# A new order table for a gated-linear-attention and spatial-gating kernel on one core

## Chip, core and metric

One core of a Trainium2 chip runs the kernel. The metric is the device time of one execution in microseconds (us). The kernel before took 139.16 us, the median of 3 runs (138.14 to 139.8). The profile is one execution of it, with a span of 137.9 us from the first to the last instruction, at a granted TensorE clock of 1.000.

Engines are named as the profile names them: PE is TensorE (matmuls), PEld its weight loads, DVE VectorE, ACT ScalarE, POOL GpSimd, and SP the engine that issues nearly all DMAs.

## What is computed

A recurrent attention is followed by a gated layer with a projection in, a spatial mix over the sequence and a projection out. Batch 4, 8 heads, sequence 768, head dimension 48, so the model dimension is 384; the hidden dimension is 1024, half of it gate.

```python
for t in range(S):                                   # _attn_ref
    state = alpha[:, :, t, :, None] * state + np.einsum('bhd,bhe->bhde', k[:, :, t], v[:, :, t])
    y[:, :, t] = np.einsum('bhd,bhde->bhe', q[:, :, t], state)
...
h = np.maximum(x @ w_in, 0.0)                        # _moe_ref, x = y with the heads side by side
u, v = (h[..., :d_ff // 2].copy(), h[..., d_ff // 2:].copy())
v_n = (v - mu) / np.sqrt(var + 1e-06)
v_s = np.einsum('ts,bsd->btd', w_spatial, v_n) + b_spatial[None, :, None]
gated = u * v_s
return (gated @ w_out).astype(np.float32)
```

## The kernel before

The sequence is cut into chunks of 128 positions, 6 to a batch and 24 in all. Inside a chunk the recurrence is written as matmuls. ACT takes the logarithm of alpha (`ln`, `lns`), PE sums it along the chunk with triangular matrices (`half`, `cum`, `cums`), ACT takes the exponential of both signs (`einv`, `eexp`), and k and q are multiplied by these (`kt` on POOL or DVE, `qt` on DVE). PE turns k and q round (`tr`, `trk`), ACT or DVE copies them out of PSUM (`ev`, `evs`), PE makes the scores (`sc`), DVE masks them (`ms`, two a chunk), and PE makes the chunk's output (`y`), adding the old state's share. The state goes from chunk to chunk by `upd` (PE), `z` (DVE), `S` (POOL or DVE) and `sb` (its bf16 copy). Chunks come in three shapes: fours (`four_chunks`, chunks 0 to 3 and 6 to 9), a pair (`pair`, chunks 4 and 5) and singles (`single`, the rest).

Each chunk's output is copied out of PSUM (`xe`). After it come, batch by batch, the projections `v` and `u` on PE with `ve` and `ue` behind them (the copies with relu), the layer norm (`bn` and `nm` on DVE, `rs` on ACT, `vn` on DVE or ACT), the spatial mix `s` (PE, in two parts of 4 and 2 matmuls, since the last two of its six row blocks come late), `se` (DVE, adds the bias), `g` (times u), the projection out `o` (PE, 4 matmuls of 384 columns), `oe` (out of PSUM) and `st` (the store). A `u`, `v`, `s` or `o` takes one PSUM bank until its reader is done with it; there are 8 banks.

The order of all this is written by hand. Every function above makes no instructions when it is called; it records operations with `op(key, engines, emit, deps, take, use)`. There are 944 of them, numbered in the order of recording. The table `PLAN` (lines 42 to 88) then says in which order and on which engine they are emitted, and `replay` (line 109) walks it. A word like `P62@0:512#0:512#0` means: operation 62 on PE, with bank 0 for the slot that it takes, and ahead of it two fillers (`warm`, line 239), matmuls of constants (`junk`) of 512 columns into bank 0, whose results nobody reads. The letters P, D, A, G and S stand for PE, DVE, ACT, POOL and SP. Each engine's words, read in the order of the table, are its program; it runs them strictly in that order, and an instruction whose inputs aren't there holds up all behind it on that engine. DMAs are issued in the order of SP's words. An operation's choice among engines is a letter of the table too.

```python
for x in junk:
    cols, kind, n = re.fullmatch("([0-9]+)([#~=])([0-9]+)", x).groups()
    ...
    warm(int(cols), int(n), kind)
...
op.emit(eng)
```

The lines that the prediction's steps touch: 242 (the fillers), 682 (`ln` of the first four chunks), 717 and 700 (`half`, `cum` and the chunk totals there), 740 and 743 (`einv`, `eexp` there), 725 (`ebc`, the exponentials of the totals), 189 (the products `kt`, `qt`, `S`, `g`), 393 (`z`), 843 and 949 (`ms`), 1067 and 1068 (`bn`), 1096 (`vn` on DVE), 178 and 180 (copies on ACT and on DVE or POOL), 184 and 186 (copies with relu on ACT and on DVE), and 1005 (all matmuls of `v`, `u`, `s` and `o`).

Of the kernel before, what the change touches and what calls it, by code (L numbers as in the profile page):

```python
# [42 lines left out]
D2 D0 D4 D1 G9 G11 G5 G6 D3 S56 S57 S59 S58 A60 S12 S169 S170 A61 S275 S171 D8 P62@0:512#0:512#0:512#0 P66@1 P67 P63  # L43
P70@2 P71 P74@3 P75 A68 A64 D79 G82 P91@4,5 P52@6 A69 A72 A76 G7 A78 A92 A84 A65 G88 G87 A73 A77 D85 D90 D81 D93 D53
D83 D80 P103@6,4,5,7:512#7:424#7 P94@0,1 D86 D104 D89 D106 G13 P97@6,2:192#2 D98 A95 P100@3,0 D101 A96 P117@3,6:376#1
P115@4,1 A99 G107 G14 A15 A173 D102 D109 P128@0,2 D119 D118 P174@5 A116 A122 A176 P130@6,4 S16 D132 D131 S172 A135
P175@1 A129 P120@3 P54@2 G110 G105 P136@0,4 A121 A178 A55 G111 G108 P133@6 G181 A180 A134 G184 A179 D112 A177 D138
P123@7,3 P141@2 S20 G279 G280 G281 G17 G19 G18 D124 D125 P151@6 P187@7,4 P126@3 S23 S277 S276 D185 A152 A127 G186 G183
G113 G114 D182 P190@5,6 A189 A192 A142 P144@3 D137 P139@4 D188 D191 A140 G22 G21 D153 D143 P199@6,5 P196@2,7 P162@4
A283 A145 P290@0 A163 P154@1 P160@3 A282 A291 A155 D200 D201 D198 D197 D164 P193@4 A161 P156@7 A157 A165 D194 D146  # L50
P158@5 A159 G195 P202@1,2 P203 S26 A204 A147 D166 P293@4 P37@5,7 D38 P34@3,6 G24 S278 S387 S399 G25 S506 S29 D35
P207@1 D148 D208 D36 A39 A292 P205 P284@7 P40@3,5 A206 A285 A167 G10 D42 P210@2 D149 D150 D41 S388 S389 D168 D209 S401
S400 P287@5 P223@6 P219@3 P221@1 A211 A294 A224 A288 D212 A286 A220 A213 D298 D304 A289 A295 D214 D222 D215 A216
P225@6 P233@2 P217@3 P229@7 P237@0 A218 A28 D301 G300 G27 D307 G297 P226 D227 G303 G306 P43@3,5 D45 P230 P234 D231
D235 A296 A44 P46@4,6 P309@5,1 D311 P238 P49@7,3 D50 D51 A48 A47 A310 P312@2,6 P318@1,4 P315@5,7 P249@3 P250 A313 A319
# [1209 lines left out]
```

## Time and profile before

| what | value |
|---|---|
| median of 3 runs | 139.16 us (138.14 to 139.8) |
| span of the profiled execution | 137.9 us |
| median less span | 1.26 us |
| PE busy | 130.1 us (94%) |
| DVE busy | 120.2 us (87%) |
| ACT busy | 107.7 us (78%) |
| POOL busy | 86.6 us (63%) |
| last instruction on PE ends | about 134.3 us |

The profile gives the span of the execution that it took and no device time of its own; the difference of 1.26 us to the median is used as what lies around the span. "Busy" counts a matmul up to its modelled end, so PE can be counted busy through short waits. A row of the timeline gives the start in us from the span's start, the time that the merged instructions cover, the engine and line, the operation, and what it writes and reads; in brackets stands the engine's idle time just before and what ended it. A row of a table by stage gives the stage, its length, and for each engine its busy time and number of instructions.

### The profile page before, as it was taken

To read this page: it belongs to the slowest core of one execution; us is meant where nothing else is said; L and a number is where in the kernel's file an instruction comes from. 1 tells how busy PE (TensorE), PEld (TensorE's weight loads), DVE (VectorE), ACT (ScalarE), POOL (GpSimd) and SP (SyncE) were. 2 spreads that over 40 slices of the span, in tenths; PEclk is the share of its full clock that TensorE was granted. 3 is DMA by queue.
4 is the path that set the end of the run, shared out by engine and by line. 5 is a ranking of instruction groups with operands and counts; after the bars stand their busy time and mean duration, and the time that the engine had idled before them with its cause. 6 is when DMAs were issued, how large, how long until landed. Compare 5 with 4: busy or idle time off the path is not lost.

```text
span 137.9 us, 5298 instructions
## 1 busy us (share of the span) xinstructions
PE 130.1 (94%) x2108; PEld 79.4 (58%) x2122; DVE 120.2 (87%) x300; ACT 107.7 (78%) x261; POOL 86.6 (63%) x146
## 2 busy tenths in 40 slices
PE   6999998999999999799999999999999999999990
PEld 3365555565566556466657676656576765566560
DVE  6259999989989999899899999997999999974960
ACT  3476998999999799699997989999865796953040
POOL 7355899993499799761079989520799841004550
PEclk9999999999999999999999999999999999999999
DMA  3999999499989788699999898999960597101064
GB/s 88 370 372 381 344 349 361 106 373 382 355 162 281 159 168 165 124 186 188 193 204 201 164 209 156 189 186 216 213 134 5 187 349 270 63 0 57 0 233 172
DMA packets 76521, 28.66 MB, mean 208 GB/s; under 512 B 63056, under 2 KB 74960, under 8 KB 76496
## 3 DMA queue, kind: packets, MB, share of 16 engines
q1 hardware_dynamic: 76464, 28.32, 77.8%
q8 instruction: 16, 0.26, 0.8%
q14 instruction: 9, 0.07, 0.2%
q0 software_dynamic: 32, 0.00, 0.0%
HBM read 23.60 MB, written 4.72 MB: 205 GB/s over the span
## 4 chain that ended last, share of the span: by engine, by line
PE 60%; DMA 19%; POOL 8%; issue 3%; SPq 3%; ACT 3%; DVE 0%; POOLq 0%; ACTq 0%
PE bank L1005 43%; DMA raw_w<-in_moe_w_spatial_dram 6%; DMA kc<-in_k_dram 5%; DMA raw_w<-in_moe_w_out_dram 4%; DMA ac<-in_alpha_dram 4%; PE bank L960 3%; SPq L883 3%; PE bank L944 2%; PE bank L988 2%; PE bank L416 2%; POOL w_row L180 2%; POOL kt L189 2%; PE bank L932 1%; PE bank L898 1%; POOL state L189 1%
## 5 line engine op out<-in xcount | busy, mean ns | idle before, releaser
L1005 PE MATMUL bank<-w_spT,vn 128*128 128x384 bf16 x192 | 35.6, 327 | 0.0
L189 POOL TENSOR_TENSOR gT<-vs,uT 128x384 bf16<-128x384 f32 x28 | 25.7, 933 | 14.1 <-DVE vs L1152 14.1
L189 POOL TENSOR_TENSOR kt<-kc,binv 128x384 bf16<-128x384 f32 x22 | 20.2, 928 | 22.3 <-ACT binv L908 15.2
L1005 PEld LDWEIGHTS <-vn 128*128 128x128 bf16 x192 | 17.5, 98 | 11.2 <-issue 0.3
L1005 PE MATMUL bank<-w_in,xT 128*128 128x512 bf16 x58 | 17.4, 380 | 1.6 <-ACT xT L178 0.7
L1005 PE MATMUL bank<-xT,w_in 128*128 128x384 bf16 x96 | 18.7, 326 | 0.0
L1005 PE MATMUL bank<-w_out_sb,gT 128*128 128x384 bf16 (+1 forms) x100 | 18.4, 320 | 0.0
L1152 DVE TENSOR_TENSOR vs<-bank,bsp_bc 128x384 f32<-128x384 f32 x31 | 16.3, 549 | 2.4 <-PE bank L1005 2.3
L949 DVE TENSOR_TENSOR ptm<-bank,mask 128x512 bf16<-128x512 f32 x28 | 17.9, 682 | 0.5 <-PE bank L944 0.3
L178 ACT COPY kqT<-bank 128x512 bf16<-128x512 bf16 (+1 forms) x20 | 15.0, 793 | 3.1 <-PE bank L988 1.9
L1067 DVE BATCH_NORM_STATS2 stats<-v_sb 128x6 f32<-128x512 bf16 x24 | 16.4, 683 | 0.6 <-ACT v_sb L184 0.5
L184 ACT ACTIVATE v_sb<-bank 128x512 bf16<-128x512 f32 x20 | 11.7, 597 | 2.0 <-PE bank L1005 1.7
L184 ACT ACTIVATE uT<-bank 128x384 bf16<-128x384 f32 x27 | 12.4, 494 | 0.7 <-PE bank L1005 0.6
L1005 PEld LDWEIGHTS <-w_in 128*128 128x128 bf16 x96 | 9.0, 97 | 6.7 <-DVE ptm L949 0.3
L189 DVE TENSOR_TENSOR qt<-qc,bank 128x384 bf16<-128x384 f32 x24 | 12.6, 545 | 0.2 <-DMA qc<-in_q_dram 0.2
L1005 PEld LDWEIGHTS <-gT 128*128 128x128 bf16 x100 | 9.2, 98 | 5.8
L178 ACT CAST xT<-bank 128x384 bf16<-128x384 f32 x23 | 10.4, 482 | 1.1 <-PE bank L416 0.8
L843 DVE TENSOR_TENSOR ptm<-bank,mask 128x512 bf16<-128x512 f32 x16 | 10.3, 683 | 0.2 <-PE bank L836 0.2
L242 PE MATMUL bank<-junk 128*128 128x512 f32 (+3 forms) x14 | 8.8, 763 | 1.0 <-DVE junk L1231 1.0
L1005 PEld LDWEIGHTS <-xT 128*128 128x128 bf16 x72 | 6.2, 97 | 6.2 <-ACT xT L178 1.2
L178 ACT COPY raw_w<-bank 128x384 f32<-128x384 f32 x8 | 3.8, 479 | 7.3 <-PE bank L1005 7.2
L393 DVE TENSOR_TENSOR zs<-bank,state 128x384 f32<-128x384 f32 x16 | 8.8, 548 | 0.5 <-PE bank L932 0.4
(162 smaller groups left out, 264.3 us busy)
## 6 DMA issues: line engine op xcount, KB each, us to landing
ac<-in_alpha_dram SPq DMA_DIRECT2D x14, 192.0 KB, 4.4
kc<-in_k_dram SPq DMA_DIRECT2D x14, 192.0 KB, 4.4
qc<-in_q_dram SPq DMA_DIRECT2D x14, 192.0 KB, 4.4
vc<-in_v_dram SPq DMA_DIRECT2D x14, 192.0 KB, 4.2
raw_w<-in_moe_w_spatial_dram SPq DMA_DIRECT2D x3, 768.0 KB, 7.8
out_dram<-raw_w SPq DMA_DIRECT2D x11, 192.0 KB, 2.1
out_dram<-o_sb SPq DMA_DIRECT2D x9, 192.0 KB, 2.0
ac<-in_alpha_dram SPq DMA_DIRECT2D x2, 768.0 KB, 6.7
```

What stands on the lines that cost most here:

```text
L178: nc.scalar.copy(out=out, in_=in_)
L184: nc.scalar.activation(out=out, in_=in_, func=AF.Relu)
L189: ENG[eng].tensor_tensor(out=out, in0=in0, in1=in1, op=ALU.mult)
L242: nc.tensor.matmul(out=banks[n][:, 0:cols].rearrange("p (a b) -> p a b", a=4), lhsT=junk, rhs=junk[:, None, 0:cols // 4].to_broadcast([128 ...
L393: lambda _: nc.vector.tensor_tensor(out=zs[i % 3], in0=tp(), in1=state[(i - 1) % 3], op=ALU.add),
L843: nc.vector.tensor_tensor(out=ptm[n2][:, ci, s], in0=banks[sl.bank].rearrange("p (hp t) -> p hp t", hp=HP), in1=mask[:, 3][:, None, :].to_ ...
L883: nc.sync.dma_start(out=t[x].rearrange("p hp s d -> p (hp s) d"), in_=src[b, :, c * C:c * C + C, :].rearrange("h s d -> s h d"))
L949: nc.vector.tensor_tensor(out=ptm[n2][:, ci, s], in0=banks[sl_p[s].bank].rearrange("p (hp t) -> p hp t", hp=HP), in1=mask[:, 2][:, None, : ...
L960: nc.tensor.matmul(out=place(to, 3 * hp + (0, 1, 1, 2)[x]), lhsT=heads(vb, hp, x), rhs=ptm[n2][:, ci, x // 2, hp, :], start=(turn == 0), s ...
L1005: nc.tensor.matmul(out=ps, lhsT=lhsT, rhs=rhs, start=first and n == 0, stop=last and n == len(pairs) - 1)
L1067: nc.vector.bn_stats(out=stats[tt % 2], in_=v_sb[n2][:, tt, :])
L1152: nc.vector.tensor_tensor(out=vs[d], in0=banks[sl.bank][:, 0:TH], in1=bsp_bc[:, th, :], op=ALU.add)
```

## The change

`PLAN` is replaced as a whole. No operation is added or removed and none is computed differently: the same 944 operations, 265 words on PE and 99 on SP in both. What differs is the order on each engine, the banks, the fillers, and the engine of some operations. In the new table DVE has 232 operations in place of 235, ACT 240 in place of 234, POOL 108 in place of 111. Of these, `ve` (v's copy with relu) is on ACT 23 times in place of 20, `sb` 6 times in place of 2, `oe` 20 times in place of 18; DVE gets two more `vn` (20 for 18), two more `ue` (7 for 5), one `xe` and one weight cast more, and gives up two `oe`, two `we`, one `ev` and one `evs`; the copies of the triangle matrices (`triq`) go from DVE to POOL.

The core of the diff, its first lines and the fillers:

```diff
 PLAN = """
-D2 D0 D4 D1 G9 G11 G5 G6 D3 S56 S57 S59 S58 A60 S12 S169 S170 A61 S275 S171 D8 P62@0:512#0:512#0:512#0 P66@1 P67 P63
...
-D83 D80 P103@6,4,5,7:512#7:424#7 P94@0,1 D86 D104 D89 D106 G13 P97@6,2:192#2 D98 A95 P100@3,0 D101 A96 P117@3,6:376#1
...
+D3 S56 S57 G11 G9 D4 D1 D0 A60 G5 G8 P62@0:512#0:512#0:512#0:512#0:512#0:264#0 P70@1 P66@2 D2 A61 P67 A68 P63 A64 P71
...
+P103@4,6,7,5:512#7:512#7:208#7 A78 D104 D80 G7 D106 P97@1,2 D98 P100@3,4:232#3 S169 A173 A99 G107 A102 P94@0,2 A96 D95
```

Three places show what the change moves. A row names the line, the operation, what it writes and reads, and the columns; numbers behind names tell tiles of one kind apart (`bank_64` to `bank_71` are the 8 PSUM banks, `binv_106` to `binv_109` the exponentials for `kt` of the first four chunks' four row groups).

The first is PE at the very start. Before, three fillers stand ahead of the first sums of the logarithms:

```order
L242 MATMUL bank_64<-junk 128x512 x3
L717 LDWEIGHTS le_quad
L717 MATMUL bank_64<-la_100,le_quad 128x384
L717 LDWEIGHTS lt_quad
L717 MATMUL bank_64<-la_100,lt_quad 128x384
L717 LDWEIGHTS le_quad
L717 MATMUL bank_65<-la_100,le_quad 128x384
```

Now there are five and a half of them, and what goes second into a bank of its own (65) is row group 2's sum in place of row group 1's:

```order
L242 MATMUL bank_64<-junk 128x512 x5
L242 MATMUL bank_64<-junk 128x264
L717 LDWEIGHTS le_quad
L717 MATMUL bank_64<-la_100,le_quad 128x384
L717 LDWEIGHTS lt_quad
L717 MATMUL bank_64<-la_100,lt_quad 128x384
L717 LDWEIGHTS le_quad
L717 MATMUL bank_65<-la_100,le_quad 128x384
```

The second place is ACT just behind these sums: `einv` (L740), `eexp` (L743), `ebc` (L725) and the copies of k (`kqT`). Before:

```order
L740 ACTIVATE binv_107<-bank_65 128x384
L740 ACTIVATE binv_106<-bank_64 128x384
L743 ACTIVATE bank_65<-bank_65 128x384
L740 ACTIVATE binv_108<-bank_66 128x384
L740 ACTIVATE binv_109<-bank_67 128x384
L725 ACTIVATE bcq_121<-bank_67 64x16 x2
L178 COPY kqT_110<-bank_68 128x4x2x64
L178 CAST o_sb_156<-vc 128x384
L743 ACTIVATE bank_64<-bank_64 128x384
L743 ACTIVATE bank_66<-bank_66 128x384
L743 ACTIVATE bank_67<-bank_67 128x384
```

Now one more exponential stands ahead of the last `einv`, and `ebc`, which stood right behind it, stands sixth behind it:

```order
L740 ACTIVATE binv_107<-bank_66 128x384
L740 ACTIVATE binv_106<-bank_64 128x384
L740 ACTIVATE binv_108<-bank_65 128x384
L743 ACTIVATE bank_65<-bank_65 128x384
L743 ACTIVATE bank_66<-bank_66 128x384
L740 ACTIVATE binv_109<-bank_67 128x384
L178 CAST o_sb_156<-vc 128x384
L178 COPY kqT_111<-bank_70 128x4x2x64
L743 ACTIVATE bank_67<-bank_67 128x384
L178 COPY kqT_110<-bank_69 128x4x2x64
L743 ACTIVATE bank_64<-bank_64 128x384
L725 ACTIVATE bcq_121<-bank_67 64x16 x2
```

The third place is DVE where the attention ends, at the last four masks (`ptm_116` with L949, chunks 22 and 23). Before, two `bn` of the last batch stand between them:

```order
L393 TENSOR_TENSOR zs_124<-bank_71,state_126 128x384
L1067 BN_STATS stats_150<-v_sb_139 128x6
L1068 BN_AGGR mvs_145<-stats_150 128x2
L180 CAST vb_114<-vc 128x8x48
L949 TENSOR_TENSOR ptm_116<-bank_71,mask 128x512
L949 TENSOR_TENSOR ptm_116<-bank_65,mask 128x512
L1067 BN_STATS stats_151<-v_sb_139 128x6
L1068 BN_AGGR mvs_145<-stats_151 128x2
L949 TENSOR_TENSOR ptm_116<-bank_68,mask 128x512
L949 TENSOR_TENSOR ptm_116<-bank_69,mask 128x512
```

Now all `bn` of the last batch stand behind the last mask:

```order
L189 TENSOR_TENSOR gT_142<-vs_152,uT_137 128x384
L949 TENSOR_TENSOR ptm_116<-bank_69,mask 128x512
L949 TENSOR_TENSOR ptm_116<-bank_65,mask 128x512
L393 TENSOR_TENSOR zs_124<-bank_66,state_126 128x384
L949 TENSOR_TENSOR ptm_116<-bank_70,mask 128x512
L949 TENSOR_TENSOR ptm_116<-bank_64,mask 128x512
L1067 BN_STATS stats_151<-v_sb_139 128x6
L1068 BN_AGGR mvs_145<-stats_151 128x2
L1067 BN_STATS stats_150<-v_sb_139 128x6
L1068 BN_AGGR mvs_145<-stats_150 128x2
```

On PE, behind the last two `y` (chunks 23 and 22), three `o` of batch 2 are left in place of one. On SP, the load of alpha for chunks 4 and 5 now stands ahead of the first load of `w_in`, and the big load of alpha for chunks 6 to 9 ahead of k's load for chunks 4 and 5; further on the loads of single chunks are in another order.

More of the change, by code (lines that the diff above doesn't have):

```diff
@@ L42 @@
 PLAN = """
[L43 to L52, printed above, removed]
@@ L83 @@
[L83 to L87 removed]
+D3 S56 S57 G11 G9 D4 D1 D0 A60 G5 G8 P62@0:512#0:512#0:512#0:512#0:512#0:264#0 P70@1 P66@2 D2 A61 P67 A68 P63 A64 P71
```

79 lines of the change are left out of this document (44 added, 35 removed).

## The prediction, on record before the run

> **What bounds the kernel now.** I read the page's busy shares first, then the table by stage, then the timeline of the start, since the new table has more fillers there. The first fence is the table by stage: length, then busy time and instructions of PE, PEld, DVE, ACT and POOL.
>
> ```profile
> 14.20:116.50 102.30, 99.45 (x1823) 62.21 (x1832) 97.61 (x221) 90.77 (x223) 73.29 (x102) 1.00 0.88 219
> 116.50:134.70 18.20, 17.77 (x160) 10.59 (x149) 13.93 (x35) 8.90 (x23) 5.26 (x20) 1.00 0.23 82
> ```
>
> The stage from 14.2 us to 116.5 us begins with DVE's first `z` and ends with its last mask. In it DVE is busy 97.61 of 102.30 us (95%) and its busy time is measured; PE shows 97%, but with modelled ends. A matmul of 384 columns lasts 327 ns in the rows, and 63 of them in a row take 10.67 us, 0.169 each (the chain's row below): half of a lone matmul's busy time is its pipeline. So in this stage DVE is at least as near its limit as PE, with ACT (89%) close behind. In the second stage, 18.2 us long, PE is busy 17.77 and DVE 13.93: there the length is PE's row of matmuls.
>
> ```profile
> 118.39 10.67 PE bank L1005 x63
> ```
>
> The start is neither. PE begins with fillers, then waits for data:
>
> ```profile
> 1.05 5.49 PE L242 MATMUL bank<-junk 128*128 128x512 f32 x6 [1.05 <-DVE junk L1231]
> 2.06 0.34 PEld L242 LDWEIGHTS bank<-junk 128*128 128x128 f32 x1 [0.52 <-issue]
> 2.92 0.34 PEld L242 LDWEIGHTS bank<-junk 128*128 128x128 f32 x1 [0.52 <-issue]
> 4.10 0.14 POOL L327 MEMSET lt_pair<- 64x64 bf16 x1
> 4.61 0.18 DVE L333 MEMSET lt_quad<- 32x16 uint32 x2
> 5.47 0.15 PEld L717 LDWEIGHTS <-le_quad 128*128 128x128 bf16 x1 [0.52 <-issue]
> 5.48 1.58 ACT L682 ACTIVATE la<-ac 128x768 bf16<-128x768 f32 x2 [3.47 <-DMA ac<-in_alpha_dram]
> 6.37 0.39 PE L717 MATMUL bank<-la,le_quad 128*128 128x384 bf16 x1
> 6.60 0.33 PE L717 MATMUL bank<-la,lt_quad 128*128 128x384 bf16 x1
> 10.71 0.19 PEld L242 LDWEIGHTS bank<-junk 128*128 128x128 f32 x1 [0.24 <-issue]
> 11.14 0.19 PEld L242 LDWEIGHTS bank<-junk 128*128 128x128 f32 x1 [0.24 <-issue]
> ```
>
> Three fillers are six passes. A pass starts each 0.86 us at first (2.06, 2.92) and each 0.43 us later (10.71, 11.14). The sixth begins at 5.47, so the fillers end near 6.33, just as ACT's first logarithm is done (5.48 and about 0.8). The first real matmul at 6.37 is followed by the next after 0.23 us and then by one each 0.16: PE came to full pace at about 6.5.
>
> **The change, part by part.**
>
> *The fillers at the start.* The new table has 5 x 512 + 264 columns ahead of the first `half`, 2.52 words more than three. Alpha's load stands first on SP as before, and the triangle matrices, whose copies go to POOL, are ready in time: POOL's two triangles end at 4.24 before, and DVE's copies of them are done 0.55 us later (4.61 and 0.18); were POOL to take two or three times as long, they would be there before 6. Nothing but the fillers then holds PE after 6.33. Passes up to 6.5 are slow as before, so the 2.52 words run at 2 x 0.43 = 0.86 us each: 2.15 us, and the first real matmul comes at 8.5. Bounds: at the slow pace throughout 2.52 x 1.71 = 4.3 us; nothing, if what PE starts has 2 us to spare.
>
> The Trainium skill ("TensorE: Matmul & The Clock Gate", Part 1) says that PE runs at half rate until about 3.4 us of sustained activity, in a window that runs freely. The doubling of pace agrees; the time here was 5.4 us after the first filler. With 3.4 us, as an estimate, the fillers would end 1.0 us sooner, at 7.5, and the sum below would be 1.0 us less.
>
> *From there to DVE's first `z`.* Has it time to spare? I follow the chain.
>
> ```profile
> 7.63 0.87 ACT L740 ACTIVATE binv<-bank 128x384 bf16<-128x384 f32 x2 [0.57 <-PE bank L717]
> 8.20 0.91 POOL L189 TENSOR_TENSOR kt<-kc,binv 128x384 bf16<-128x384 f32 x1 [3.46 <-ACT binv L740]
> 9.63 0.49 ACT L740 ACTIVATE binv<-bank 128x384 bf16<-128x384 f32 x1 [0.35 <-PE bank L700]
> 10.02 0.36 ACT L725 ACTIVATE bcq<-bank 64x16 f32<-64x16 f32 x2
> 11.05 0.91 POOL L189 TENSOR_TENSOR kt<-kc,binv 128x384 bf16<-128x384 f32 x1
> 12.46 0.78 PE L794 MATMUL bank<-o_sb,kt 32*128 32x96 bf16 x56 [0.24 <-POOL o_sb L180]
> 13.26 0.56 DVE L189 TENSOR_TENSOR state<-bank,bcq 128x384 f32<-128x384 f32 x1
> 13.74 0.54 DVE L189 TENSOR_TENSOR qt<-qc,bank 128x384 bf16<-128x384 f32 x1
> 14.20 0.55 DVE L393 TENSOR_TENSOR zs<-bank,state 128x384 f32<-128x384 f32 x1
> ```
>
> ACT waited for PE's sums (0.57), POOL for ACT (3.46), PE at 12.46 for the last of POOL, so a late PE passes straight on; nothing is to spare. In the new order ACT's first `einv` needs the eighth matmul, as before, so it comes 2.15 later with some 0.2 more for the pipeline: about 10.0. ACT starts an exponential each 0.41 us. Five of them precede the last `einv`, at 12.1 (9.63 before); its `kt` on POOL is done at 13.5 (11.96 before), where the big masks of POOL no longer stand in its way, and `upd` ends at 14.3. But `S` (13.26 before) also needs `ebc`, which now stands sixth behind that `einv`: after a cast, two copies and two exponentials ACT is at 14.8 and done at 15.15. Then DVE does `S` at 15.2, one `qt` at 15.65, `z` at 16.15. That is **+1.95 us**. The range for it is 0 (the chain has spare time after all) to 4.3.
>
> *The stage of DVE's load.* Between the first `z` and the last mask the new table has 188 operations on DVE in place of 190. All `ms`, `se`, `z` and `qt` are the same number. The others, with mean ns from DVE's groups by form:
>
> ```profile
> L1067 DVE BATCH_NORM_STATS2 stats<-v_sb 128x6 f32<-128x512 bf16 x24 | 16.4, 683 | 0.6 <-ACT v_sb L184 0.5
> L1096 DVE TENSOR_SCALAR vn<-v_sb,mvs,rstd 128x512 bf16<-128x512 bf16 x18 | 6.9, 404 | 0.0
> L1068 DVE BATCH_NORM_AGGREGATE mvs<-stats 128x2 f32<-128x6 f32 x24 | 4.4, 182 | 0.8
> L180 DVE COPY kqT<-bank 128x1024 bf16<-128x1024 bf16 x5 | 3.3, 680 | 0.3 <-PE bank L988 0.3
> L186 DVE TENSOR_SCALAR uT<-bank 128x384 bf16<-128x384 f32 x5 | 2.8, 552 | 0.3 <-PE bank L1005 0.3
> L186 DVE TENSOR_SCALAR v_sb<-bank 128x512 bf16<-128x512 f32 x4 | 2.7, 672 | 0.0
> L180 DVE COPY w_spT<-bank 128x384 bf16<-128x384 bf16 x8 | 2.6, 352 | 0.5 <-ACT rstd L1077 0.4
> L180 DVE COPY o_sb<-bank 128x384 f32<-128x384 f32 x2 | 1.1, 554 | 0.1
> L180 DVE CAST xT<-bank 128x384 bf16<-128x384 f32 x1 | 0.5, 524 | 0.0
> L180 DVE CAST vb<-vc 128x384 bf16<-128x384 f32 x1 | 0.3, 327 | 0.0
> ```
>
> Fewer: two `bn` (2 x 0.865 = 1.73), two `we` (0.70), one `evs` (0.68), two `ve` (1.34), one `ue` (0.55), three `oe` (1.66): 6.66 us. More: three `vn` (1.21), two `xe` (1.05), one `vbs` (0.33), and one each of a `vp` (as an `xe`, 0.52), a weight cast (0.45, between the casts' 0.33 and 0.52) and a `g` (as a `ue`, 0.55): 4.11 us. That is 2.55 us less. DVE starts the next instruction before the last has ended (13.26 with 0.56, the next at 13.74), so an instruction is worth about 0.9 of its duration: 2.3 us, and at 95% busy **-2.4 us** of the stage. Bounds: nothing (another engine holds the stage at its length) and 2.55.
>
> *PE behind the last `y`.* One `o` of batch 2 was left there, now three: 8 matmuls more, at 0.169 us **+1.35 us**, on PE's row that sets the end. These matmuls leave the stage before, where PE is not the tighter engine; were they free there as well as here, the term would be nothing.
>
> *ACT.* It gets more `ve` (3), `sb` (4), `oe` (2), `we` (2), `ev` and `evs`, and gives up two `vn`, two `ue`, an `xe`, a `vp` and a `vbs`. With
>
> ```profile
> L184 ACT ACTIVATE v_sb<-bank 128x512 bf16<-128x512 f32 x20 | 11.7, 597 | 2.0 <-PE bank L1005 1.7
> L178 ACT COPY kqT<-bank 128x1024 bf16<-128x1024 bf16 x9 | 9.0, 1016 | 2.0 <-PE bank L988 1.9
> L1092 ACT ACTIVATE vn<-v_sb,shift,rstd 128x512 bf16<-128x512 bf16 x6 | 4.9, 815 | 0.2 <-DVE shift L1084 0.2
> ```
>
> and about 0.5 us for each of the others that is about 3.3 us more of duration, 2.9 of busy time. In the stage it would come from 90.8 to at most 93.7 us, below DVE's 97.6 - 2.2 = 95.4. So I cost it at nothing; its cover is 1.7 us thin.
>
> *Loads, POOL, banks.*
>
> ```profile
> 13.78 0.61 POOL L180 CAST w_in<-raw_w 128x512 bf16<-128x512 f32 x1 [1.37 <-DMA raw_w<-in_moe_w_in_dram]
> 18.55 1.79 POOL L189 TENSOR_TENSOR kt<-kc,binv 128x384 bf16<-128x384 f32 x2
> 19.74 0.34 PE bank L1005
> GB/s 88 370 372 381 344 349 361 106 373 382 355 162 281 159 168 165 124 186 188 193 204 201 164 209 156 189 186 216 213 134 5 187 349 270 63 0 57 0 233 172
> ```
>
> The loads of alpha moved up put 0.39 and 0.79 MB ahead of the first `w_in` and of k for chunks 4 and 5. At the some 370 GB/s of the page's first slices that is 1.1 and 2.1 us. The first `w_in` landed at 13.78, and the first `v` ran at 19.74 (the chain's row); k's was first used at 18.55, and its `kt` now stands behind two of the long products on POOL that followed it. Both are hidden, the second by some 2 us; without that cover they cost what they are late. POOL gives up about 1 us, was busy 72% of the stage and bounds nothing. New banks change which reader a matmul waits for; I cost them at nothing, since PE's hidden waits have no row of their own, and keep half a per cent either way.
>
> **Sum.** 1.95 - 2.4 + 1.35 = +0.9 us on the profiled span of 137.9: 138.8, and with the 1.26 us by which the median stands above that span, 140.1 us (+0.7%).
>
> **Rivals.** *ACT takes DVE's place (slower).* If the stage can't shrink, because ACT, which starts 2.4 us late and has 3 us more to do, feeds DVE and PE late, DVE's saving is lost: 137.9 + 1.95 + 1.35 = 141.2, a time of 142.4 us (+2.4%). For it speaks that PE, DVE and ACT are all at 89% or more in the stage; against it that ACT stays 1.7 us below DVE. It decides from the point where ACT's busy time in the stage reaches DVE's.
>
> *The start is made good (faster).* If PE reaches full pace sooner, or chunks 0 to 3 overlap better behind `z`, the start costs nothing and the three engines have 2.4 us less to the last mask: 137.9 - 2.4 + 1.35 = 136.9, 138.1 us (-0.8%); with the two `o` free besides, 136.8 us (-1.7%). For it speaks that the table still has 1464 columns of filler behind the first sums (1504 before), so PE has room there; against it that the chain above has no slack in it.
>
> *The order does nothing.* With the same work on engines so evenly loaded the terms could cancel: 139.2 us. This lies inside the forecast's own range, 139.0 to 141.2.
>
> **How the numbers follow.** I give the forecast 0.40, ACT's rival 0.32, the start's rival 0.28. A per cent, 137.8 to 140.55, is about what a measurement of this kernel can tell from no change. Of the forecast about two thirds lie within it and a third above; ACT's rival lies above; of the start's, somewhat over half lies below and the rest within. So faster 0.19, same 0.36, slower 0.45. The range for 8 in 10 runs from 137.0 (the start made good, half of the two `o` free) to 143.2 (ACT's rival, with the start 0.8 dearer).
>
> **What would show it.** Right: the first L717 matmul at about 8.5 us, `ebc` near 14.8, DVE's first `z` near 16.2, its last mask near 116.0, then 19.5 us to PE's end. Wrong: a first `z` before 15.2, a stage from `z` to last mask of 102 us or more (ACT's rival, with ACT busier than DVE), or PE gaps of over 1 us behind 20 us.

## The result, and the profile after

The changed kernel takes **143.97 us** (median of 5 runs, 142.59 to 146.1) against 139.05 us before (5 runs, 138.14 to 139.8): 3.5% more by the medians, and 1.031 as the ratio of the comparable runs, 95% interval 1.023 to 1.039. The prediction was 140.1 us, in a range of 137.0 to 143.2; the measured time lies above that range. The profiled execution has a span of 142.2 us and a mean granted clock of 0.975; its time was 143.97 us, so 1.8 us lie around the span. (Two of the five runs, at a granted clock of 1.0, took 142.59 and 142.83 us; the ratio leaves out those of 144.9 and 146.1 us, which count as slow because they are over 1.5% above the fastest.)

The table by stage, cut where the prediction cut it: from DVE's first `z` to its last mask, and from there to PE's end (length, then busy time and instructions of PE, PEld, DVE, ACT and POOL, granted clock, DMA share, GB/s).

```profile
16.07:118.60 102.53, 100.40 (x1798) 61.65 (x1801) 97.67 (x216) 92.86 (x227) 71.56 (x96) 0.97 0.85 208
118.60:138.60 20.00, 19.56 (x171) 11.41 (x169) 16.07 (x39) 9.53 (x24) 6.41 (x22) 1.00 0.26 95
```

The first stage did not get shorter: 102.53 us after 102.30. The prediction had 99.9 for it. DVE's busy time there is 97.67 us, as much as before, although the prediction had counted 2.55 us of durations less (where they went stands in the section on why it was wrong). ACT, at 92.86 us, stayed below DVE.

Rows picked from the timeline of the changed kernel, from the fillers to the first `v` (start, time covered, engine, line; in brackets the idle time just before and what ended it):

```profile
7.22 1.04 PE L242 MATMUL bank<-junk 128*128 128x512 f32 x3
8.09 0.33 PE L717 MATMUL bank<-la,le_quad 128*128 128x384 bf16 x1
...
9.59 1.25 ACT L740 ACTIVATE binv<-bank 128x384 bf16<-128x384 f32 x3 [2.49 <-PE bank L717]
...
14.74 0.37 ACT L725 ACTIVATE bcq<-bank 64x16 f32<-64x16 f32 x2 [0.57 <-DVE qt L189]
15.14 0.56 DVE L189 TENSOR_TENSOR state<-bank,bcq 128x384 f32<-128x384 f32 x1 [0.44 <-ACT bcq L725]
...
16.07 0.55 DVE L393 TENSOR_TENSOR zs<-bank,state 128x384 f32<-128x384 f32 x1
18.62 2.86 DVE L843 TENSOR_TENSOR ptm<-bank,mask 128x512 bf16<-128x512 f32 x4 [0.34 <-ACT bsp_bc L178]
...
24.07 0.61 PE L1005 MATMUL bank<-w_in,xT 128*128 128x512 bf16 x1
```

Up to `z` the marks are near where the prediction put them: first real matmul 8.09 (8.5), `ebc` 14.74 (14.8), `z` 16.07 (16.15). Then comes what it had not looked at. The first masks start 2.55 us behind `z`; before they start 2.04 us behind it. The first `v`, at 19.71 us before, comes at 24.07.

```profile
14.20 0.55 DVE L393 TENSOR_TENSOR zs<-bank,state 128x384 f32<-128x384 f32 x1
...
16.24 2.53 DVE L843 TENSOR_TENSOR ptm<-bank,mask 128x512 bf16<-128x512 f32 x4
...
19.71 1.57 PE L1005 MATMUL bank<-w_in,xT 128*128 128x512 bf16 x5
```

These three are rows of the kernel before. In the same place the granted clock (the column behind POOL's) falls in the changed kernel, here in stretches of 3.41 us, the first four rows of a table by stage:

```profile
12.35:15.76 3.41, 3.41 (x88) 2.06 (x86) 2.97 (x7) 2.81 (x8) 2.38 (x6) 1.00 1.07 391
15.76:19.17 3.41, 3.16 (x69) 1.92 (x69) 2.97 (x7) 3.32 (x8) 2.37 (x5) 1.00 1.15 339
19.17:22.58 3.41, 3.17 (x54) 1.83 (x52) 3.22 (x6) 2.97 (x9) 3.41 (x5) 0.50 1.00 323
22.58:26.00 3.42, 3.20 (x54) 1.83 (x50) 3.21 (x7) 2.28 (x5) 3.42 (x6) 0.50 0.71 235
```

For 6.8 us PE runs at half clock, and it is "busy" for 93% of them. In the kernel before the column shows 1.00 in all four.

To see where the time goes I use landmarks: the start of an operation's first matmul in the trace. One thing must be known of the kernel before: its profiled execution (span 137.9 us, so some 139.7 us with the 1.8 around it) was one of its slower ones. It holds a wait for a load of alpha at 57.4 us that passes on to PE:

```profile
57.41 0.52 ACT L888 ACTIVATE la<-ac 128x384 bf16<-128x384 f32 x1 [1.09 <-DMA ac<-in_alpha_dram]
...
58.85 0.35 PE L960 MATMUL bank<-ptm,vb 128*32 128x128 bf16 x12 [1.03 <-ACT uT L184]
```

No profile of a later kernel with that order shows it. The second row of the table below, a kernel before with four instructions of DVE's left out that made no difference to the time (next section), stands in for an undisturbed execution.

| us from the span's start | first real matmul | first `z` | `y` 0 | `y` 3 | `y` 4 | `y` 22 | last `o` | from `y` 4 to last `o` |
|---|---|---|---|---|---|---|---|---|
| before, profiled | 6.37 | 14.20 | 17.91 | 23.46 | 29.04 | 116.70 | 133.82 | 104.78 |
| before, less DVE | 6.33 | 14.16 | 17.87 | 23.42 | 28.91 | 115.25 | 132.37 | 103.46 |
| after | 8.09 | 16.07 | 22.77 | 27.62 | 33.50 | 119.27 | 137.72 | 104.22 |

Against the second row the last `o` comes 5.35 us later: 1.91 are lost by the first `z`, 2.68 more between `z` and `y` 4, and 0.76 behind it (0.57 gained up to `y` 22, 1.33 lost from there). Another 0.45 us go behind PE's last matmul, from whose end to the span's end it is 3.99 us where it was 3.54; what causes that was not followed.

### The profile page after: what moved, and what is told of

It reads as the page before. It is cut to its first block, busy times and chain, and to the rows that moved or that the text cites. A ratio compares the mean times of both kernels' runs of the same rounds, so it can differ in the third digit from the quotient of the medians.

```text
span 142.2 us, 5298 instructions
## 1 busy us (share of the span) xinstructions
PE 134.9 (95%) x2116; PEld 81.1 (57%) x2128; DVE 121.4 (85%) x292; ACT 111.1 (78%) x267; POOL 87.3 (61%) x148
## 4 chain that ended last, share of the span: by engine, by line
PE 74%; ACT 12%; DVE 9%; issue 2%; DVEq 0%; ACTq 0%
PE bank L1005 46%; PE bank L242 5%; PE bank L944 3%; ACT kqT L178 3%; PE bank L416 2%; PE bank L836 2%; PE bank L960 2%; PE bank L988 2%; DVE zs L393 2%; PE bank L854 2%; DVE qt L189 2%; ACT uT L184 2%; DVE kt L189 1%; DVE state L189 1%; PE bank L898 1%
## 5 line engine op out<-in xcount | busy, mean ns | idle before, releaser
L1005 PE MATMUL bank<-w_spT,vn 128*128 128x384 bf16 x192 | 36.1, 327 | 0.3 <-DVE vn L1096 0.3
L189 POOL TENSOR_TENSOR kt<-kc,binv 128x384 bf16<-128x384 f32 x22 | 20.8, 958 | 19.3 <-ACT binv L908 14.8
L1005 PE MATMUL bank<-xT,w_in 128*128 128x384 bf16 x96 | 19.6, 327 | 0.0
L1005 PE MATMUL bank<-w_in,xT 128*128 128x512 bf16 x60 | 18.3, 394 | 0.8 <-issue 0.2
L1005 PE MATMUL bank<-w_out_sb,gT 128*128 128x384 bf16 (+1 forms) x100 | 18.4, 320 | 0.3 <-DVE zs L393 0.3
L178 ACT COPY kqT<-bank 128x512 bf16<-128x512 bf16 (+1 forms) x22 | 16.7, 792 | 2.0 <-PE bank L988 1.7
L949 DVE TENSOR_TENSOR ptm<-bank,mask 128x512 bf16<-128x512 f32 x28 | 17.6, 680 | 0.2 <-ACT xT L178 0.2
L184 ACT ACTIVATE v_sb<-bank 128x512 bf16<-128x512 f32 x23 | 13.9, 611 | 1.9 <-PE bank L1005 1.8
L184 ACT ACTIVATE uT<-bank 128x384 bf16<-128x384 f32 x25 | 11.8, 501 | 3.3 <-PE bank L1005 3.2
L178 ACT CAST xT<-bank 128x384 bf16<-128x384 f32 x22 | 9.9, 486 | 3.0 <-PE bank L416 1.4
L242 PE MATMUL bank<-junk 128*128 128x512 f32 (+3 forms) x20 | 10.2, 659 | 1.0 <-DVE junk L1231 1.0
L178 ACT COPY raw_w<-bank 128x384 f32<-128x384 f32 x11 | 5.1, 482 | 4.9 <-PE bank L1005 4.7
```

The source lines that it names most:

```text
L178: nc.scalar.copy(out=out, in_=in_)
L184: nc.scalar.activation(out=out, in_=in_, func=AF.Relu)
L189: ENG[eng].tensor_tensor(out=out, in0=in0, in1=in1, op=ALU.mult)
L242: nc.tensor.matmul(out=banks[n][:, 0:cols].rearrange("p (a b) -> p a b", a=4), lhsT=junk, rhs=junk[:, None, 0:cols // 4].to_broadcast([128 ...
L949: nc.vector.tensor_tensor(out=ptm[n2][:, ci, s], in0=banks[sl_p[s].bank].rearrange("p (hp t) -> p hp t", hp=HP), in1=mask[:, 2][:, None, : ...
L1005: nc.tensor.matmul(out=ps, lhsT=lhsT, rhs=rhs, start=first and n == 0, stop=last and n == len(pairs) - 1)
```

## The experiments

The expectations of the four runs that come first in time (two on each kernel, with fillers added or taken away) set the clock and the start against each other. The later ones use letters for the theories. **D** is the prediction's: DVE sets the pace from `z` to the last mask. **P**: PE's own row of matmuls sets it, so moving DVE's load does nothing and PE's work can be moved but not hidden. **H**: the loss lies in the head, by chunk 3's `y`. **R**: the new order behind the head costs. Inside the head: **W** (the late `ebc`) and **M** (the order of scores, masks and first `v`).

**The clock and the start.** The first runs hold the clock up with more fillers, and then take the long start away:

```diff
-P175@6 A178 P54@4 A55 D101 P128@1,0 A129 A135 P130@2,3 D109
+P175@6 A178 P54@4:256=4 A55 D101 P128@1,0:256=1 A129 A135 P130@2,3:256=2 D109
...
-P123@1,2 A122
+P123@1,2:256=1:256=1 A122
```

> The new table with eleven more fillers (two bf16 matmuls of 256 columns each) between 17.5 and 22.5 us, where PE has only scores, transposes and outputs of 32 to 64 rows or columns. Clock theory: the granted clock of 0.5 from 19.2 to 26.0 us in the new table's profile comes from too little work on the array in the window before it; the fillers keep it at 1.000 in every execution, and the time is that of the executions without the drop, 142.2 to 143.0 us. Order theory: the clock is only a symptom, the waits behind the first z are the order's own, and the time stays at 143 to 145 us even where the clock stands at 1.000.

Measured: 144.5 us, ratio 1.045 (1.039 to 1.051). The clock stayed at full until PE's work was done, and nothing was gained.

> The same with three fillers at the very start in place of five and a half, as before the change. Start theory: the first real matmul comes at 6.4 us in place of 8.1, DVE's first z at 14.4 in place of 16.1, and the time is 1.7 us below that of the kernel with fillers alone. Rival: behind z other waits (loads, the masks on DVE) take the gain up, and the time is within 0.5 us of it.

Measured: 142.35 us, ratio 1.030 (1.025 to 1.035), 2.15 us less than the run above by the medians. In the two profiled executions the 2.52 words of filler cost less: the first real matmul comes 1.30 us sooner (6.29 for 7.59), `z` 1.01 and the last `o` 1.16; the rest of the difference lies behind PE's end. Then the same start without the other fillers:

```diff
-P62@0:512#0:512#0:512#0:512#0:512#0:264#0 P70@1
+P62@0:512#0:512#0:512#0 P70@1
```

> The changed kernel with three fillers at the start in place of five and a half, nothing else. The prediction's first term: 1.95 us less than the changed kernel (143.97 us), 142.0 us. Theory H with the granted clock full throughout: 142.7 - 2.15 = 140.5 us; with the clock at half for a while behind 17 us, 141.5 to 142.3 us.

Measured: 141.77 us, ratio 1.022 (1.018 to 1.026), 2.2 us less than the changed kernel's median, but only 0.8 to 1.1 less than its two runs at a clock of 1.0; in the profiles `z` comes 1.23 us sooner. Here the clock falls again; the table by stage from 14.8 us of the run with fillers and of this one:

```profile
14.80:18.20 3.40, 3.18 (x53) 1.74 (x51) 2.07 (x6) 3.14 (x7) 2.91 (x5) 1.00 1.13 342
18.20:21.60 3.40, 3.40 (x68) 1.95 (x66) 2.99 (x6) 2.67 (x8) 3.40 (x5) 1.00 0.99 315
21.60:25.00 3.40, 3.35 (x66) 1.70 (x66) 3.33 (x8) 3.10 (x8) 3.01 (x6) 1.00 0.98 325
```

```profile
14.80:18.20 3.40, 2.96 (x66) 1.70 (x59) 2.96 (x8) 3.34 (x8) 2.63 (x5) 1.00 1.13 345
18.20:21.60 3.40, 3.06 (x77) 1.83 (x80) 3.12 (x6) 3.33 (x9) 3.40 (x5) 0.78 1.10 366
21.60:25.00 3.40, 3.40 (x39) 1.50 (x36) 3.40 (x7) 2.18 (x6) 3.40 (x6) 0.71 0.84 271
```

Yet chunk 3's `y` starts at 25.55 us in the one and at 25.54 in the other, 2.1 us later than before in both. This pair alone does not part the clock from the order, since eleven pairs of fillers, 0.11 us a matmul, are themselves some 2.4 us of work for PE. The times of the last run's four executions say more: at a mean clock of 1.0 and 0.998, without the drop, they are 141.97 and 141.66 us, at 0.986 and 0.983, with it, 141.88 and 141.0. Without the added fillers and at full clock this kernel is still some 3 us above the 138.79 us that the kernel before took beside it, so the clock alone isn't the rest of the loss.

The same two levers on the kernel before:

```diff
-P62@0:512#0:512#0:512#0 P66@1
+P62@0:512#0:512#0:512#0:512#0:512#0:264#0 P66@1
```

> The kernel before with the five and a half fillers of the new table at its start and nothing else changed. Start theory: the first real matmul at 8.1 us in place of 6.4 and the time 1.7 us above before, 140.8 us. Rival, that the start has time to spare: within 0.4 us of before.

Measured: 141.94 us, ratio 1.021 (1.013 to 1.030). `z` comes 2.13 us later and `y` 3 3.31 us later. The start's price was the forecast's up to `z` and grew behind it: PE stands still twice in the middle of a group, 0.45 us at 20.52 and 0.71 at 25.90, for nothing that the profile shows, which is the 1.2 us more.

```diff
-P103@6,4,5,7:512#7:424#7 P94@0,1 D86 D104 D89 D106 G13 P97@6,2:192#2 D98 A95 P100@3,0 D101 A96 P117@3,6:376#1
+P103@6,4,5,7 P94@0,1 D86 D104 D89 D106 G13 P97@6,2 D98 A95 P100@3,0 D101 A96 P117@3,6
```

> The kernel before without its three groups of fillers behind the first sums (936, 192 and 376 columns), which leaves only small matmuls and waits from 9.5 to 17 us. Clock theory: the granted clock drops to 0.5 for some 7 us in the stretch from 13 to 25 us, and the time rises by 1 to 3 us. Rival, that fillers there are worth nothing: clock 1.000 and time within 0.5 us of before.

Measured: 142.5 us, ratio 1.023 (1.014 to 1.032). The clock is at half for three stretches:

```profile
14.40:17.80 3.40, 2.79 (x50) 1.41 (x49) 3.15 (x7) 3.24 (x8) 2.79 (x6) 0.52 1.12 347
17.80:21.20 3.40, 3.40 (x67) 2.10 (x67) 2.44 (x4) 2.32 (x8) 2.48 (x4) 0.50 1.01 314
21.20:24.60 3.40, 3.18 (x27) 1.26 (x26) 2.80 (x5) 1.36 (x4) 3.24 (x5) 0.50 1.05 350
```

So those fillers are what keeps the kernel before at full clock, and losing it costs that kernel some 3 us (2.3% by the ratio): `y` 0 comes 0.86 us later and `y` 4 3.26.

**DVE or PE.** One run takes from DVE what the change was forecast to take, and nothing else; its mirror gives PE more to do.

```diff
-            nc.vector.bn_stats(out=stats[tt % 2], in_=v_sb[n2][:, tt, :])
+            if (b, tt) not in ((1, 1), (1, 4), (2, 1), (2, 4)):
+                nc.vector.bn_stats(out=stats[tt % 2], in_=v_sb[n2][:, tt, :])
```

> The kernel before without four of its 24 BN_STATS on DVE (batches 1 and 2, positions 1 and 4: their layer norms use an old row's statistics), 4 x 0.683 = 2.7 us of DVE's load inside the stage from first z to last mask, with nothing else moved. Theory P: PE sets the pace there, so 138.0 to 138.5 us, no change. Theory D: DVE sets the pace, so the stage shrinks by 0.9 x 2.7 = 2.5 us, 135.8 us.

Measured: 138.72 us (10 runs) beside 138.35, ratio 1.001 (0.997 to 1.004): no change. The stage from `z` to the last mask and the one behind it:

```profile
14.16:115.05 100.89, 100.33 (x1836) 62.06 (x1832) 95.08 (x217) 90.60 (x223) 73.19 (x102) 1.00 0.90 223
115.05:133.25 18.20, 17.82 (x161) 10.60 (x149) 13.94 (x35) 8.91 (x23) 5.27 (x20) 1.00 0.20 73
```

DVE is 2.53 us less busy than in the prediction's row (95.08 for 97.61) and PE is busy 100.33 of 100.89 us, 99%. Most of the 1.4 us by which the stage is shorter than in the prediction's row is the wait for the load (1.03 us on PE), absent here; from `y` 4 to the last `o` three executions with all of DVE's load there and no such wait have 103.48, 103.52 and 103.68 us, this one 103.46. So 2.7 us of DVE's work are worth 0.2 us at most.

```diff
-P524@2,0
+P524@2,0:256=2
...
-P640@0,2
+P640@0,2:256=0
```

> The kernel before with twelve matmuls of constants more on PE (six pairs of 256 columns, 0.115 us each by the rows of such fillers in an earlier run, 1.35 us in all) between 60 and 92 us, at places where the bank that they write had been free for over 1.2 us, so that they wait for nothing. It is the mirror of the run with less of DVE's load. Theory P (PE sets the pace): 138.3 + 1.35 = 139.7 us. Theory D (DVE sets it, PE has room): 138.3 to 138.6 us.

Measured: 140.67 us beside 138.67, ratio 1.013 (1.008 to 1.019). From `y` 4 to the last `o` it has 105.14 us, 1.68 more than 103.46. 1.35 us of matmuls that nothing waits for cost all of their time and a little more. Theory D falls, and P holds, in the stretch that these two runs change, 57 to 93 us. Neither run touches the head: there, between 14.2 and 24.4 us, DVE is busy for 10.04 of 10.20 us in the kernel before and PE for 9.46.

**PE's work behind the last `y`.** Two of the three `o` go back ahead of it:

```diff
-D856 A704 S705
+D856 A704 P706@1 S705
...
-A821 A818 A811 P824@2
+A821 A818 A811 P712@5 P824@2
```

> The changed kernel with two of the three matmul groups o of batch 2 that it leaves behind the last y put back ahead of them (o of row 2 behind chunk 19's y, o of row 4 ahead of the last u of that stage), their copies and stores with them. By the prediction's third term PE's stretch from the last y to its end gets 1.35 us shorter and the stage before it does not get longer: 1.3 us less than the changed kernel in all. Theory P: PE has no room in the stage before, so the last y comes 1.3 us later and the time does not change (within 0.3 us of the changed kernel at the same clock, 142.6 to 144).

Measured: 145.66 us (143.64 to 146.59), ratio 1.040 (1.029 to 1.051). From `y` 22 to the last `o` 17.93 us (18.45 in the changed kernel), from `y` 4 to `y` 22 87.13 us (85.77). The profiled execution is that of 146.59 us, with a wait of 2.3 us ahead of `y` 4, so only the stretches behind it are compared, and both forecasts of the time are missed. The two `o` come back in full, 1.36 us, ahead of the last `y`: PE has no room there. At the end only 0.52 us of them are saved, for the `v` behind `y` 22 now waits 0.58 us for ACT's copy of that `y`, a wait that one of these `o` had filled.

**Where the loss lies: spliced tables.** Each follows one kernel's order up to a moment and the other's behind it. The first two were made with banks given anew in the head as well.

```diff
-P103@6,4,5,7:512#7:424#7
+P103@6,4,5,7:512#6:424#6
```

> The order of the kernel before for every operation that starts there before 29.5 us (up to chunk 4's y), then the order and engines of the changed kernel for all the rest; banks are given anew where the two don't meet. Theory P (PE's own row sets the pace from chunk 0's y to the end, and all of the loss lies ahead of chunk 3's y): the changed order behind chunk 4 is worth about +0.9 us of PE waits, so about 139.2 us (138.3 to 140). Theory D, as predicted (DVE sets the pace, and the new order takes 2.4 us from it, with 1.35 us given back behind the last y): 138.3 - 2.4 + 1.35 = 137.2 us. Theory R (the changed order behind chunk 4 is itself a cause of the loss): 141 us or more.

Measured: 143.19 us, ratio 1.032 (1.026 to 1.039). The line above is why this run decides nothing: two fillers in the middle of the head now go into the bank that DVE still reads, and wait for it.

```profile
11.76 1.84 PE L242 MATMUL bank<-junk 128*128 128x512 f32 x4 [1.41 <-DVE bsp_bc L180]
```

`z` comes 1.15 us later than before, though up to there the order is the same and only banks were changed.

> The reverse: the changed kernel's order for every operation that starts there before 34.0 us (up to chunk 4's y, with its 5.5 fillers), then the order and engines of the kernel before. Theory P: chunk 4's y comes 4.4 us later than before and nothing makes it good: 141.8 to 142.7 us. Theory D: only the start's 1.95 us are lost ahead of DVE's first z, and DVE has its old load behind it: 140.3 us.

Measured: 144.18 us, ratio 1.042 (1.033 to 1.050), with a `z` at 18.20 us in place of 16.07: the same flaw, again 1.4 us of waiting for `bsp_bc`. Both were made again, cut at chunk 3's `y`, with the head's banks left alone. The first words that differ from the kernel whose head it is:

```diff
-G18 D124 D125 P151@6 P187@7,4 P126@3
+D124 D125 P151@6 P187@7,4 P126@3 D185
```

> As the first of the spliced tables, but cut earlier and with the banks and fillers of the head left as they stand: the kernel before's order for what starts there before 24.0 us (up to chunk 3's y), then the changed kernel's order, engines and banks for the rest. Theory H (the loss lies in the head: fillers, and chunks 0 to 3 with their masks finished ahead of the first v): chunk 3's y at 23.5 us as before, then the changed kernel's own 110.1 us to PE's end in place of some 109.0, so 139.4 us (138.6 to 140.2). Theory R (the changed order behind the head is what costs): 141.5 us or more. The prediction's DVE term: 137.2 us.

Measured: 141.03 us, ratio 1.018 (1.015 to 1.022). `y` 3 stands at 23.43 us as before. Right behind the splice PE waits for a cast of w_in that POOL does later in the other order:

```profile
25.07 0.99 PE L1005 MATMUL bank<-xT,w_in 128*128 128x384 bf16 x5 [0.78 <-POOL w_in L180]
```

Of the 2.0 us lost behind `y` 3 (110.94 to the last `o`, 108.95 in the kernel with less DVE) 1.37 are lost by `y` 4, where this wait of 0.78 is, and 0.63 behind it. The time lies between H's range and R's, so neither number is met; without the splice's own wait it would be near H's.

> The reverse at the same place, banks and fillers of the head left as they stand: the changed kernel's order for what starts there before 28.2 us (up to chunk 3's y), then the kernel before's. Theory H: chunk 3's y at 26.2 us (PE's clock full) to 27.6 us (at half for a while, as in the changed kernel's profile), then 109.0 us to PE's end and 5.9 to the time: 141.1 to 142.6 us. Theory R: 139 us or less. The prediction: only the start's 1.95 us, 140.3 us.

Measured: 144.34 us, ratio 1.042 (1.038 to 1.045). `y` 3 comes at 28.70 us, and from `y` 4 to the last `o` the kernel before's order takes 103.52 us. The changed kernel's head alone is enough for all of its loss, which is H's claim and against R's 139 us or less. H's own number is missed: `y` 3 comes 1.1 us later than in the changed kernel, 0.54 of it by `z` (its fillers ended later) and the rest with a wait of PE of 0.8 us that has no releaser in the profile.

> The kernel before's order for what starts there before 53.1 us (up to chunk 8's y), then the changed kernel's. Theory P (PE's row sets the pace, whichever order it is in): from chunk 8's y to PE's end 79.9 us as in the changed kernel, against 80.2 before: 138.0 us (137.6 to 138.6). The prediction's DVE term would take some 60% of 2.4 us off and give 1.35 back, 138.2 us, so this run does not tell these two apart; it tells whether any part of the new order is worth having: a time under 137.6 us would say so.

Measured: 141.34 us, ratio 1.021 (1.017 to 1.025). From `y` 8 to `y` 10, right behind the splice, it takes 7.72 us in place of 5.19; a splice there costs too much for the question, and the run settles nothing.

Over all runs the last column of the table above is nearly a constant of the order. The kernel before's order has 103.46, 103.48, 103.52 and 103.68 us from `y` 4 to the last `o`, whatever stood ahead of it; the changed one 104.09 (behind before's head), 104.19 (three fillers) and 104.22. Two runs with fillers changed (104.55 before's order, 104.70 the changed one) and the first two splices (104.91 and 106.26) lie above, as do the runs whose work there was changed. So the new order behind the head costs 0.4 to 0.8 us and gains nothing.

**What the rest of the head's loss is.** W's run puts `ebc` back, where with three fillers it waited for a product of DVE's that reads the same bank,

```profile
13.50 0.37 ACT L725 ACTIVATE bcq<-bank 64x16 f32<-64x16 f32 x2 [0.96 <-DVE qt L189]
```

and one product on DVE ahead of `S`:

```diff
-D85 A76 A81
+D85 A76 A78 A81
...
-A78 D104 D80 G7 D106
+D80 D104 G7 D106
```

> The changed kernel with three fillers at the start, and with ebc back right behind the last einv on ACT and the product qt of the first row group ahead of S on DVE, as the kernel before has them. Without the second edit ebc starts at 13.50 us there, after a wait of 0.96 for a product of DVE's that reads the same bank. Theory W (this wait is the rest of the head's loss): z comes 0.5 us sooner and that qt 1.0 us, chunk 3's y at 24.5 to 25.0 us in place of 25.54, and the time is 140.8 to 141.3 us. Theory M (the order of scores, masks and the first v behind z is what costs): chunk 3's y stays at 25.3 to 25.6 us, and the time at 141.6 to 141.9 us.

Measured: 142.58 us, ratio 1.027 (1.023 to 1.031), 0.8 us more than without the edit. `z` does come 0.51 us sooner, and `y` 3 0.90 us later, at 26.44. Neither W's numbers nor M's are met. An earlier `z` did not end the head sooner, but the run is no clean test of W: its clock is at half for 6.8 us (18.4 to 25.2) in place of 3.4 (20.1 to 23.6), and PE stands 0.7 us for nothing that the profile shows.

> The kernel before's order for what starts there before 15.5 us (fillers, sums, exponentials, ebc, upd, z, the turning of k and q of chunks 0 to 3), then the changed kernel's order, engines and banks from the scores on. Theory W: the scores start as before, at 15.6 us, chunk 3's y comes at 23.4 to 24.2 us, and the time is that of the splice at chunk 3's y, 140.7 to 141.4 us. Theory M: chunk 3's y comes at 25 us or later, and the time is 142 us or more.

Measured: 142.31 us, ratio 1.027 (1.020 to 1.035). `z` at 13.96, `y` 3 at 25.38: M's numbers, but not M's proof, because of a wait that the splice made.

```profile
16.26 0.48 PE L466 MATMUL bank<-la,le_pair 128*128 128x384 bf16 x2 [1.75 <-ACT la L448]
```

The last run has no splice. PE's order behind `upd` in the kernel before and in this run, by the operations' names (`pm` brings v into order for `vb`, `bb` makes the bias of the spatial mix, `cum:2` are sums of chunks 4 and 5):

```diff
-tr:q:0 tr:k:1 tr:q:1 sc:0 pm:0 pm:2 cum:2:0 sc:2 cum:2:1 y:0 bb:1 sc:3 y:2 sc:1 v:0:0 v:0:2 tr:k:2 y:1 tr:q:2 v:0:1 y:3
+tr:k:1 tr:q:1 tr:q:0 pm:2 sc:2 pm:0 cum:2:0 sc:1 cum:2:1 sc:0 bb:1 y:2 sc:3 y:0 y:1 v:0:2 tr:k:2 v:0:0 tr:q:2 v:0:1 y:3
```

> The kernel before, with its fillers, ebc and engines, in which only the words of chunks 0 to 3 behind the first upd (turning and copies of k and q, scores, copies of v, masks, y, the first v) stand in the changed kernel's relative order: 13 words of PE, 12 of DVE, 11 of ACT and 3 of POOL change places, banks are given anew where they must. Theory M (this order is what the rest of the head's loss comes from): first z at 14.2 us as before, chunk 0's y at 20 us or later in place of 17.9, chunk 3's y at 25 us or later in place of 23.4, and 140 us or more. Rival (the order of these chunks is made good by chunk 3's y, and the loss is that of fillers and ebc alone): chunk 3's y at 23.4 to 24.2 us, and 138.3 to 139.2 us.

Measured: 144.88 us, ratio 1.046 (1.042 to 1.051). `z` stands at 13.96 us, `y` 0 at 24.16, `y` 3 at 30.04, and from `y` 4 on it has 103.48 us like the kernel before. PE's timeline there, and the clock:

```profile
15.81 0.35 PE L814 MATMUL bank<-o_sb,ident 32*32 32x384 bf16 x8 [0.66 <-ACT kqT L178]
...
17.56 0.32 PE L466 MATMUL bank<-la,le_pair 128*128 128x384 bf16 x1 [0.57 <-ACT la L448]
...
19.19 1.62 PE L242 MATMUL bank<-junk 128*128 128x376 f32 x2
20.74 0.61 PE L836 MATMUL bank<-kqT 48*128 48x128 bf16 x8
...
22.14 0.62 PE L854 MATMUL bank<-ptm,vb 128*32 128x128 bf16 x16 [0.36 <-DVE ptm L843]
```

```profile
19.50:22.90 3.40, 3.04 (x39) 1.40 (x38) 1.51 (x3) 0.00 (x0) 0.14 (x1) 0.50 1.05 350
22.90:26.30 3.40, 3.04 (x63) 1.79 (x55) 2.24 (x5) 2.94 (x9) 2.15 (x3) 0.50 0.46 181
```

An order of 39 words, with the start, `ebc` and the engines as before, is enough to lose 6.4 us, most of it (some 5 us) while the clock is at half, from 18.9 to 29.2 us. It is more than in the changed kernel (2.3 us from `z` to `y` 3), since here the words around them are not made for it, and three things keep it from being a proof of M. The filler of 376 columns is tied to `sc` 0 and so moved from 14.73 to 19.19 us, where it takes 1.62 us at half clock; the run without fillers showed what that clock does without them. The banks of 200 words of PE are new, and `pm` 2, whose input was ready by 12.2 us, waits 0.66 us for ACT's copy of the q that had been turned, which can only be the emptying of its bank. And `cum` waits 0.57 us for ACT's `ln`, which comes 1.1 us later than before, as the copies ahead of it do. So the order of these words matters as much as M says; whether by its own waits or by leaving the clock without dense work is not shown, and its share in the changed kernel is not measured by this run.

None of the sixteen kernels is faster than the kernel before.

## Why the prediction was wrong, step by step

*The fillers at the start, +1.95 us.* Right in mechanism, and in size partly by luck: `z` came 1.9 us later. On the way three differences nearly cancel. The first real matmul came at 8.09 where I had 8.5; `ebc` then waited 0.57 us for a `qt` of DVE's, which I had not; and `upd`, forecast to end at 14.3, ended at 15.0, behind fillers ahead of it that keep PE until 14.15. The fillers' price isn't a constant either: three pairs of profiles that differ in them put `z` 1.01, 1.23 and 2.13 us apart. With the same 5.5 fillers the first real matmul stands at 7.59, 7.69, 8.09, 8.58, 8.63 and 8.77 us in six executions, since a pass takes 0.86 us up to about 4.5 us in the first of these and up to about 6.9 in the last. The Trainium skill ("TensorE: Matmul & The Clock Gate", Part 1) says that the window that opens the clock runs freely and isn't reset by the kernel; this spread of 1.2 us agrees.

*The stage of DVE's load, -2.4 us.* This is the step that failed. I took a busy time of 95% on DVE for a limit and discounted PE's 97%, because its ends are modelled. That 97% held the wait for a load, which was that one execution's; without it PE is busy 99%, and the view of its waits from 29 to 116 us is empty. PE was the limit where the runs reach (57 to 93 us), and by its waits from `y` 4 to `y` 22: less work on DVE bought 0.2 us at most, more on PE cost all of it. From `z` to `y` 22 the change gave not -2.4 us but +2.1: +2.29 from `z` to `y` 3, +0.39 to `y` 4, and -0.57 behind it, the last although two `o` of 0.65 us each had left that stretch.

The work taken from DVE was mis-sized besides. I priced each instruction at its mean in the kernel before, which gave 2.55 us less; in the changed kernel's stage the durations on DVE add up to 112.1 us where they were 112.4. Two of its `vn` take 1.00 us where every `vn` before took 0.38 to 0.41, one `S` takes 1.23 where the five before took 0.55 to 0.65, and a cast of v 0.83 for 0.33. Each of these four runs while POOL is at products or casts for nearly all of its length; that POOL is the cause was not tested.

*The head behind `z`.* It has no term in the sum. I followed the chain up to the first `z` and then priced 100 us by counting DVE's instructions; the order itself, which is the whole of the change, was priced at nothing behind `z`. There the new order does the masks of three chunks before the first `y` 0 and puts the first `v` behind all of it, so that between the last filler at 15.9 us and 24 us PE has, but for a handful of 384 columns, only small matmuls, and the clock halves. How the 2.3 us divide between the order's own waits and the clock stays open: with three fillers at the start the executions without the drop were no faster than those with it, while between executions of the changed kernel a clock of 1.0 goes with 142.6 to 142.8 us and one of 0.975 with 143.97.

*PE behind the last `y`, +1.35 us.* Right in size, 1.33 us, but for a reason that should have changed the step before: if PE's row is the limit at the end and in the stage before it, these matmuls are not an extra cost. Moved back, two of them cost the same there (1.36 us).

*ACT, POOL and loads, 0.* No wait of note came from them in the changed kernel; all of PE's waits in its profile but one at the very start:

```profile
PE bank L1005 <- DVE zs L393: 0.3, 1, 0.3
PE bank L1005 <- DVE vn L1096: 0.3, 1, 0.3
PE bank L1005 <- issue: 0.2, 1, 0.2
PE bank L771 <- ACT kqT L178: 0.2, 1, 0.2
```

One microsecond in all: an engine that hardly waits is the bound. That view of the kernel before, with PE's one long wait in it (1.0 us, for the load) and 1.5 us of others, would have said so. ACT's rival had made ACT's busy time in the stage reaching DVE's its condition; it did not (92.86 and 97.67 us).

*Banks, 0.* The cost was small but not nothing. `ebc` reads the totals in the bank from which DVE's `qt` reads its exponentials, and it waited 0.57 us for DVE, since its place is now behind that `qt`. The Trainium skill ("PSUM — Partial Sum Buffer", PSUM bank collisions raise a hardware error) says that even two readers on different engines must be kept apart by bank and quadrant; the wait agrees, though a semaphore of the program makes it, not the chip.

*The sum's base.* The terms were added to one execution that held a wait of 1.1 us, and 1.26 us were taken for what lies around the span where it is 1.8. The two errors cancel by half in the forecast time, but they hid that the undisturbed kernel has no such wait to give back.

The rival with the slower end, ACT in DVE's place, came nearest in time (142.4) and was wrong in its cause: PE had the place, and had had it before.

## What to carry to other kernels

Before pricing a load moved off one engine, ask which engine waits least in the stage, with the waits of that one execution (a late load) set aside; modelled ends make PE's busy share uncertain, but its list of waits tells. On a bound engine moved work is neither gained nor lost, so a term that charges it where it arrives and credits nothing where it left is a sign of a mistake. A mean duration in the old order need not be the price in the new one: two `vn` took 1.00 us there in place of 0.40. And where a change is an order, the stretch in which little dense work is at hand (here 8 us behind the first state) is to be walked through instruction by instruction: what stood first in line there decided more than the sum of durations.

## What the runs showed of the hardware

The granted clock fell to 0.50 while PE was busy 93% of the time and waited nowhere more than 0.3 us (19.17 to 26.0 us in the changed kernel), during and behind a stretch of mostly small matmuls: 48 rows by 128 columns, 32 by 32 tiles, transposes of 64 by 64. In the kernel before fillers of full size, 1504 columns in all, keep it up through the same operations; without them it was at 0.50 to 0.52 for 10.2 us. The Trainium skill ("TensorE: Matmul & The Clock Gate", HAM oscillation) has idle gaps of over 3.4 us as what closes the gate; here there was none. The busy share of the profile doesn't tell either: the 3.41 us ahead of the drop (15.76 to 19.17) are busy for 3.16 us, while the kernel before keeps the full clock with 2.84 us of 3.42 (22.58 to 26.00). Whether the size of the matmuls counts, the transposes among them, or gaps that modelled ends hide, no run here separates. That a drop lasts whole stretches of about 3.41 us (one in the changed kernel with three fillers, two in the changed kernel, three without fillers) agrees with its window.

A filler is not free of waits: moved into a bank whose reader was not done, two fillers held PE 1.41 us.
